# Attention with an MLP mixer on one core: score products over all 32 rows of a head slot, the exponent offset as a product of constants, a six-step VectorE exponential, set-up fills moved

## The chip, the cores and the metric

The kernel runs on one core of one Trainium2 chip. The metric is the device time of one execution in microseconds (us), as the median of several runs. A profile of one further execution gives the rows shown here; its time stands beside the median below. TensorE (PE) does the matrix products, ScalarE (ACT) and VectorE (DVE) work on their results, SyncE (SP) issues the transfers. TensorE's clock is granted in one of two levels, 1.2 and 2.4 GHz, which the profile writes as 0.5 and 1.0 of full speed.

## The reference

```python
xn = _layernorm(A_x)                                   # (1, 2048, 640) bf16
def _A_ref(x, wqkv, wo):                               # H = 32 heads of Dh = 20
    qkv = ((x @ wqkv).reshape(B, S, 3, H, Dh)).transpose(2, 0, 3, 1, 4)
    q, k, v = qkv[0], qkv[1], qkv[2]
    scores = jnp.einsum("bhqd,bhkd->bhqk", q, k) * (Dh ** -0.5)
    p = _softmax(scores, axis=-1)
    o = jnp.einsum("bhqk,bhkd->bhqd", p, v)
    return o.transpose(0, 2, 1, 3).reshape(B, S, D) @ wo
def _B_ref(x, w1, b1, w2, b2):                         # an MLP over the 2048 positions, 1536 wide
    h = _layernorm(x)
    u = _gelu(jnp.einsum("bsd,sf->bdf", h, w1) + b1)
    return (jnp.einsum("bdf,fs->bds", u, w2) + b2).transpose(0, 2, 1)
return A_x + _A_ref(xn, A_wqkv, A_wo) * _silu(_B_ref(xn, B_w1, B_b1, B_w2, B_b2))
```

## The kernel before

The 32 heads are worked in eight groups G of four. A group's q and k are made by products with `wqkvp_sb`, whose columns are spread so that each head has a slot of 32 rows in `qk_sb`: 20 rows of the head and 12 that hold whatever follows it in the weights. The step that takes them out of PSUM (`ev_fn`, L878 on VectorE, L877 on ScalarE in the first microseconds) multiplies and adds a number for each row (columns of `cst_sb`): it scales q, sets the spare rows of q and k to zero, and puts into the first spare row the constant 49152 (`OFFS`) on q's side and 1 on k's.

The attention is cut into 2048 units: a unit is one head, one block of 512 queries and one block of 128 keys. `emit_st` writes a unit's score product (L920): 128 keys by 512 queries into one PSUM bank, with the head's 20 rows as contraction. Two to five score products stand next to each other in the order, on different groups of 32 rows of the array, so that they run side by side. PSUM's eight banks: 0 to 2 and 3 and 4 are the two groups that ScalarE's exponential (L945) empties three or two units at a time into `pt_sb`; bank 5 is VectorE's; bank 6 collects the value products; bank 7 serves all other products.

About one unit in eleven has its exponential on VectorE. Its score product takes 21 rows, so that the constant adds 49152 to the score. VectorE then computes the exponential with seven instructions on 128 by 512 values (`start_dchain`, L984 to L991): it takes the low 16 bits of the score with its offset (`ew_sb`), builds a correction from them (`ev_sb`, `es_sb`, `el_sb`) and adds it to the score to give the bits of a bfloat16 number (`dpt_sb`). `emit_pv` writes the value products (L1025): the exponentials of a unit as moving operand, 32 columns of `v_sb` (a column of ones and the head's 20 values among them) as weights, four heads side by side.

Beside the attention run the MLP's products (L674), the products for later groups (L598), and near the end the output products (L736, L742). Their results leave PSUM on VectorE.

The order of instructions on every engine is fixed when the program is built. `schedule` simulates the engines with costs for each instruction and takes, step after step, the candidate that is ready first, by priority. It also keeps a model of TensorE's clock (`_Gate`): each product adds a number of columns to a running count, 512 for a full product, `512 * 0.156` for a score product and `512 * 0.25` for a value product, and where the count runs low the planner puts in products of constants whose result nobody reads (`warm_step`, L1387, operands from `wrm_sb`). Nothing of this model is known to the chip.

At the start VectorE fills constants: `wrm_sb`, bank 6, the identity, four small columns of `cst_sb`, the ones and gaps of `v_sb` (L499, L501), `on_sb` and `wo7_sb` (L502, L503; `wo7_sb` reads as `wo_sb` in rows of the profile). Then come the layer norm's statistics (L522, L524, L527).

Of the kernel before, what the change touches and what calls it, by code (L numbers as in the profile page):

```python
# [10 lines left out]
P = 128  # L11
# [28 lines left out]
class _Gate:  # L40
# [235 lines left out]
class _Kern:  # L276
# [6 lines left out]
    RP = 25  # L283
    VB = 724
# [36 lines left out]
    def build(self):  # L321
# [4 lines left out]
        with es:  # L326
# [20 lines left out]
            sb("wrm_sb", [P, 512], bf)  # L347
# [3 lines left out]
            sb("es_sb", [P, nd], bf)  # L351
# [25 lines left out]
    def schedule(self):  # L377
# [8 lines left out]
        ew_sb, ev_sb, es_sb, el_sb = t["ew_sb"], t["ev_sb"], t["es_sb"], t["el_sb"]  # L386
# [48 lines left out]
        def dma(fn, reads, writes, name, nbytes, tag=None):  # L435
            pr.dma(fn, reads=reads, writes=writes, name=name, cost=1800.0 + nbytes / 170.0)
# [24 lines left out]
        def small(fn):  # L461
            def f(e):
# [14 lines left out]
        pr.dve(lambda e: e.memset(wrm_sb[:], 1.0), writes=[S_("warm")], name="warm1", cost=240)  # L477
# [3 lines left out]
        selap = bass.AP(idf_sb, DH, [[P, P], [32, GH]])  # L481
        pr.dve(lambda e: e.tensor_reduce(cst_sb[:, 0:1], selap, mybir.AxisListType.X, ALU.add), reads=[S_("idf")],
               writes=[S_("bk")], name="bk", cost=150)
        CQ0 = self.LOG2E * 128.0 / math.sqrt(float(DH))
        pr.dve(lambda e: e.tensor_scalar(cst_sb[:, 1:2], cst_sb[:, 0:1], self.OFFS, None, ALU.mult),
               reads=[S_("bk")], writes=[S_("bq")], name="bq", cost=150)
        pr.dve(lambda e: e.tensor_scalar(cst_sb[:, 3:4], cst_sb[:, 0:1], -1.0, 1.0, ALU.mult, ALU.add),
               reads=[S_("bk")], writes=[S_("ck")], name="ck", cost=150)
        pr.dve(lambda e: e.tensor_scalar(cst_sb[:, 4:5], cst_sb[:, 0:1], -CQ0, CQ0, ALU.mult, ALU.add),
               reads=[S_("bk")], writes=[S_("cq")], name="cq", cost=150)  # L490
# [5 lines left out]

        for h0, nh in ((0, 8), (8, 24)):
            onesap = bass.AP(v_sb, voff(h0), [[NB * VB, P], [VB, NB], [22, nh], [21, 2]])
            pr.dve(lambda e, ap=onesap: e.memset(ap, 1.0), writes=[S_("v_ones")], name="v_ones", cost=100.0 + NB * nh * 2)  # L499
            gapap = bass.AP(v_sb, voff(h0 + nh - 1) + 22, [[NB * VB, P], [VB, NB], [1, 10]])  # L500
            pr.dve(lambda e, ap=gapap: e.memset(ap, 0.0), writes=[S_("v_ones")], name="v_gap", cost=240)  # L501
# [979 lines left out]
```

## Time and profile before

| | |
|---|---|
| median of 3 runs | 1028.91 us (1022.38 to 1039.81) |
| the profiled execution's own time | 1025.38 us |
| its span, from the first to the last instruction | 1023.6 us |
| mean granted clock of TensorE over the span | 0.851 |
| busy: TensorE, ScalarE, VectorE | 90%, 87%, 76% of the span |
| instructions | 15713 |

Busy shares are of the whole span. The kernel's stretches have different limits, so the rows below take stretches apart: one at the high clock level, one at the low level and some in between. A matrix product's busy time is modelled at its end and overlaps with its neighbours, so a busy TensorE may still have room.

### The profile page before, as it was taken

The numbers are of one execution on the slowest core, as the hardware profiler recorded it, in microseconds if no ns is written. First come the engines' busy times: TensorE is split into PE (matmuls) and PEld (weight loads), VectorE is DVE, ScalarE is ACT, GpSimd is POOL, SyncE is SP. The second block draws the span as 40 slices with busy tenths as digits, with TensorE's granted clock in tenths as the row PEclk, the third lists the DMA queues.
The fourth block names the chain that finished last, engine by engine and source line by source line (L and its number), as shares of the span: only waits on it lengthen the run. The fifth ranks groups of instructions, "written<-read, shape, count | busy, mean of one in ns | idle before, by whom it ended". The sixth has DMA issues, their size and how long they took to land.

```text
span 1023.6 us, 15713 instructions
## 1 busy us (share of the span) xinstructions
PE 916.9 (90%) x5972; PEld 273.8 (27%) x5972; DVE 779.8 (76%) x1874; ACT 887.9 (87%) x782; POOL 13.0 (1%) x31
## 2 busy tenths in 40 slices
PE   7889788899899898898999998888898899789997
PEld 4432222222222222222222222222222222322222
DVE  7878889867787878877658877886878767676665
ACT  3799999988999988998978989999999988787773
POOL 1400000000000000000000000000000000000000
PEclk9899999957989969988758889998989978885557
DMA  7030000000010101000020110101101012300001
GB/s 225 8 89 6 6 6 6 7 28 20 6 47 7 47 1 48 6 6 6 7 61 7 37 37 6 32 5 38 36 6 36 6 39 70 96 1 26 1 26 52
DMA packets 42203, 30.69 MB, mean 30 GB/s; under 512 B 4707, under 2 KB 41571, under 8 KB 42131
## 3 DMA queue, kind: packets, MB, share of 16 engines
q1 hardware_dynamic: 42131, 29.70, 9.7%
q8 instruction: 49, 0.80, 0.3%
q14 instruction: 23, 0.19, 0.1%
HBM read 23.40 MB, written 6.29 MB: 29 GB/s over the span
## 4 chain that ended last, share of the span: by engine, by line
PE 45%; DVE 28%; ACT 22%; issue 4%; POOL 0%; DVEq 0%; POOLq 0%
ACT pt_sb L945 21%; PE ps_all L920 15%; PE ps_all L1025 9%; PE ps_all L674 8%; DVE ew_sb L984 5%; PE ps_all L1387 5%; PE ps_all L598 4%; PE ps_all L736 4%; DVE dpt_sb L991 3%; DVE es_sb L987 3%; DVE qk_sb L878 3%; DVE el_sb L990 3%; DVE ev_sb L985 2%; DVE es_sb L989 2%; DVE el_sb L988 1%
## 5 line engine op out<-in xcount | busy, mean ns | idle before, releaser
L945 ACT ACTIVATE pt_sb<-ps_all 128x1536 bf16<-128x1536 f32 x743 | 863.1, 1257 | 103.8 <-PE ps_all L920 99.6
L920 PE MATMUL ps_all<-qk_sb 20*128 20x512 bf16 (+1 forms) x2048 | 358.6, 433 | 66.0 <-ACT pt_sb L945 35.7
L984 DVE TENSOR_SCALAR ew_sb<-ps_all 128x512 uint16<-128x512 uint16 x192 | 131.3, 684 | 132.3 <-PE ps_all L920 132.1
L1025 PE MATMUL ps_all<-pt_sb,v_sb 128*32 128x512 bf16 x1856 | 189.3, 441 | 0.0
L920 PEld LDWEIGHTS ps_all<-qk_sb 20*128 20x128 bf16 (+1 forms) x2048 | 82.7, 93 | 381.0 <-ACT pt_sb L945 209.0
L991 DVE SCALAR_TENSOR_TENSOR dpt_sb<-ps_all,el_sb 128x512 uint16<-128x512 f32 x192 | 132.2, 689 | 5.4
L1387 PE MATMUL ps_all<-wrm_sb 128*128 128x512 bf16 (+1 forms) x356 | 104.2, 404 | 11.4 <-DVE qk_sb L878 7.1
L598 PE MATMUL ps_all<-xnT_sb,wqkvp_sb 128*128 128x512 bf16 x320 | 101.4, 415 | 9.8 <-DVE wqk_sb L682 3.7
L674 PE MATMUL ps_all<-regB,regA 128*128 128x512 bf16 (+1 forms) x384 | 83.4, 341 | 4.8 <-DVE qk_sb L878 4.7
L990 DVE TENSOR_TENSOR el_sb<-es_sb,el_sb 128x512 bf16<-128x512 bf16 x192 | 81.5, 425 | 6.2
L987 DVE TENSOR_TENSOR es_sb<-ev_sb 128x512 bf16<-128x512 bf16 x192 | 81.1, 422 | 5.3
L1025 PE MATMUL ps_all<-dpt_sb,v_sb 128*32 128x512 bf16 x192 | 84.2, 446 | 0.0
L674 PE MATMUL ps_all<-regC,regA 128*128 128x128 bf16 (+1 forms) x384 | 80.6, 342 | 2.2 <-DVE qk_sb L878 2.2
L878 DVE TENSOR_SCALAR qk_sb<-ps_all,cst_sb 128x512 bf16<-128x512 f32 x60 | 48.2, 804 | 14.6 <-PE ps_all L598 14.5
L985 DVE TENSOR_SCALAR ev_sb<-ew_sb 128x512 bf16<-128x512 uint16 x192 | 55.4, 288 | 4.7
L989 DVE TENSOR_SCALAR es_sb<-es_sb 128x512 bf16<-128x512 bf16 x192 | 55.2, 287 | 0.0
L988 DVE TENSOR_SCALAR el_sb<-ev_sb 128x512 bf16<-128x512 bf16 x192 | 54.8, 285 | 0.0
L1025 PEld LDWEIGHTS ps_all<-pt_sb,v_sb 128*32 128x32 bf16 x1856 | 35.8, 97 | 67.5 <-issue 52.3
L1387 PEld LDWEIGHTS ps_all<-wrm_sb 128*128 128x128 bf16 x356 | 34.6, 111 | 62.6 <-DVE qk_sb L878 12.8
L736 PE MATMUL ps_all<-wo_sb,xnT_sb 120*128 120x512 bf16 (+3 forms) x160 | 44.6, 408 | 2.1 <-DVE regC L752 2.1
L674 PEld LDWEIGHTS ps_all<-regC,regA 128*128 128x128 bf16 x384 | 30.8, 111 | 46.5 <-issue 34.0
L598 PEld LDWEIGHTS ps_all<-xnT_sb,wqkvp_sb 128*128 128x128 bf16 x320 | 25.8, 101 | 64.5 <-issue 13.3
(68 smaller groups left out, 395.9 us busy)
## 6 DMA issues: line engine op xcount, KB each, us to landing
regA<-in_B_w_dram SPq DMA_DIRECT2D x6, 1024.0 KB
regA<-in_B_w_dram SPq DMA_DIRECT2D x8, 768.0 KB
regA<-in_A_x_dram SPq DMA_DIRECT2D x7, 640.0 KB
oT_scratch_dram<-stage_sb SPq DMA_DIRECT2D x28, 128.0 KB
xnT_sb<-oT_scratch_dram SPq DMA_DIRECT2D x4, 480.0 KB
out_dram<-regC SPq DMA_DIRECT2D x3, 640.0 KB
wqk_sb<-in_A_wqkv_dram SPq DMA_DIRECT2D x2, 800.0 KB
wv_sb<-in_A_wqkv_dram SPq DMA_DIRECT2D x1, 800.0 KB
```

The lines of the kernel that those rows point to most:

```text
L598: steps.append(("pe", lambda e, dc=dc: e.matmul(ps(bk), wqkvp_sb[:, dc, w, G, :], xnT_sb[:, dc, tb * 512:(tb + 1) * 512], start=(dc == 0), ...
L674: steps.append(("pe", lambda e, k=k: e.matmul(ps(bk, n), wap[:, k, col0:col0 + 128], rows[:, k, c0:c0 + n], start=(k == 0), stop=(k == nk ...
L736: steps.append(("pe", lambda e, c=c, k=k: e.matmul(ap, oT_sb[0:k, c, b * 128:(b + 1) * 128], wo_sb[0:k, c, c0:c0 + n], start=(c == 0), sto ...
L878: return lambda e: e.tensor_scalar(dst, src, sc, bias, ALU.mult, ALU.add)
L920: pr.pe(lambda e, outp=outp, lhsT=lhsT, rhs=rhs, g=g: e.matmul(outp, lhsT, rhs, start=True, stop=True, tile_position=(32 * g, 0)), reads=[ ...
L945: tk = pr.act(lambda e: e.activation(outp, inp, AF.Exp, scale=math.log(2.0) / 128.0), reads=[bank_slot[b] for b in banks[:n]], writes=[S_( ...
L984: (lambda e: e.tensor_scalar(w3, lo, 0x7FFF, None, ALU.bitwise_and), bs, [S_("ew")], dv(N)),
L987: (lambda e: e.tensor_tensor(s_, v_, v_, ALU.mult), [S_("ev")], [S_("es")], dv(N, .52)),
L990: (lambda e: e.tensor_tensor(l_, s_, l_, ALU.mult), [S_("es"), S_("el")], [S_("el")], dv(N, .52)),
L991: (lambda e: e.scalar_tensor_tensor(o_, zr, -(self.OFFS - 16256.0), l_, ALU.add, ALU.add), bs + [S_("el")], [S_(f"dpt{s0 + i}") for i in r ...
L1025: pr.pe(lambda e, outp=outp, lhsT=lhsT, rhs=rhs, k=k, g=g: e.matmul(outp, lhsT, rhs, start=(k == 0), stop=(k == NB - 1), tile_position=(0, ...
L1387: pe_full(lambda e: e.matmul(ps(wb, n), wrm_sb[:, 0:P], wrm_sb[:, 0:n], start=True, stop=True), [S_("warm")], [bank_slot[wb]], "warm", n)
```

## The change

Score products take all 32 rows of the slot (L910 of the changed kernel). Only q's spare rows are set to zero, by a scale without an addition; k's spare rows keep what the weights gave, and k is copied as it is. The offset of VectorE's units is written into bank 5 ahead of the score product by a full product of constants over 128 rows (`prime`, L1313): 128 rows of 1 by 128 rows of 49152/128. The score product then adds to it (`start=not dvex`). The planner takes a priming product when bank 5 is free, and a VectorE unit only in a primed bank.

VectorE's exponential becomes six steps: the correction is built as a product of two linear functions of `ew_sb` and of `ew_sb` itself, and `es_sb` is gone. One of its products now multiplies a bfloat16 by a 16-bit whole number.

The planner's model of the clock counts `512 * 0.25` columns for a score product. Its costs for transfers are other numbers as well (`DMA0`, `DMAB`). The fills of `v_sb`, `on_sb` and `wo7_sb` become jobs that the planner places after the first normalised blocks, and the first value products wait for the fill of `v_sb` (`c01`).

```diff
-            sb("wrm_sb", [P, 512], bf)
+            sb("wrm_sb", [P, P + 512], bf)
...
-        pr.dve(lambda e: e.memset(wrm_sb[:], 1.0), writes=[S_("warm")], name="warm1", cost=240)
+        pr.dve(lambda e: e.memset(wrm_sb[:, 0:P], 1.0), writes=[S_("warm1")], name="warm1", cost=100)
+        pr.dve(lambda e: e.memset(wrm_sb[:, P:P + 512], self.OFFS / P), writes=[S_("warm")], name="warm", cost=200)
...
-            return lambda e: e.tensor_scalar(dst, src, sc, bias, ALU.mult, ALU.add)
+            return lambda e: e.tensor_scalar(dst, src, sc, None, ALU.mult)
...
-                kk = DH + 1 if dvex else DH
-                lhsT = qk_sb[32 * g:32 * g + kk, slot, 1, c * 128:(c + 1) * 128]
-                rhs = qk_sb[32 * g:32 * g + kk, slot, 0, p * 512:(p + 1) * 512]
+                lhsT = qk_sb[32 * g:32 * g + 32, slot, 1, c * 128:(c + 1) * 128]
+                rhs = qk_sb[32 * g:32 * g + 32, slot, 0, p * 512:(p + 1) * 512]
...
+                    outp, lhsT, rhs, start=not dvex, stop=True, tile_position=(32 * g, 0)),
...
-            pr.gate.add(pr.T["pe"], n * 512 * 0.156)
+            pr.gate.add(pr.T["pe"], n * 512 * 0.25)
...
-                (lambda e: e.tensor_scalar(v_, w_, 1.0 / 256.0, -64.0, ALU.mult, ALU.add), [S_("ew")], [S_("ev")],
+                (lambda e: e.tensor_scalar(v_, w_, 1.0 / 256.0, -128.0, ALU.mult, ALU.add), [S_("ew")], [S_("ev")],
                  dv(N, .26)),
-                (lambda e: e.tensor_tensor(s_, v_, v_, ALU.mult), [S_("ev")], [S_("es")], dv(N, .52)),
-                (lambda e: e.tensor_scalar(l_, v_, a3, b3, ALU.mult, ALU.add), [S_("ev")], [S_("el")], dv(N, .26)),
-                (lambda e: e.tensor_scalar(s_, s_, -4096.0, None, ALU.add), [S_("es")], [S_("es")], dv(N, .26)),
-                (lambda e: e.tensor_tensor(l_, s_, l_, ALU.mult), [S_("es"), S_("el")], [S_("el")], dv(N, .52)),
+                (lambda e: e.tensor_scalar(l_, w_, a3 / 65536.0, (b3 - 64.0 * a3) / 256.0, ALU.mult, ALU.add),
+                 [S_("ew")], [S_("el")], dv(N, .26)),
+                (lambda e: e.tensor_tensor(l_, v_, l_, ALU.mult), [S_("ev"), S_("el")], [S_("el")], dv(N, .52)),
+                (lambda e: e.tensor_tensor(l_, l_, w_, ALU.mult), [S_("el"), S_("ew")], [S_("el")], dv(N, .52)),
...
+        add_job("consts", cs[:2] + [("tag", "c01")], ("xn_g0",), 21.0)
+        add_job("consts2", cs[2:], ("xn_g1",), 24.5)
...
+        def prime(dg):
+
+            for b in dg:
+                pe_full(lambda e, b=b: e.matmul(ps(b), wrm_sb[:, 0:P], wrm_sb[:, P:P + 512], start=True, stop=False),
+                        [S_("warm"), S_("warm1")], [bank_slot[b]], "offs", 512)
+            dgrp_state[dg] = "primed"
```

The planner gives a new order. Three places of it follow. The first is VectorE at the start of the program, from the last small constant to the layer norm's first statistics. Before:

```order
L491 MEMSET wqk_sb 128x8
L499 MEMSET v_sb 128x16x8x2
L501 MEMSET v_sb 128x16x5
L499 MEMSET v_sb 128x16x24x2
L501 MEMSET v_sb 128x16x5
L502 MEMSET on_sb 128x256
L503 MEMSET wo_sb 128x320
L522 BN_STATS bst_sb<-regA 128x6
```

The same place of the changed kernel, where L514 and L516 are the statistics:

```order
L489 TENSOR_SCALAR cst_sb<-cst_sb 128x1
L491 MEMSET wqk_sb 128x8
L514 BN_STATS bst_sb<-regA 128x6
L516 BN_STATS bst_sb<-regA 128x6
L519 BN_AGGR st_sb<-bst_sb 128x2
```

Six fills have left the stretch ahead of the statistics; they stand after the first normalised blocks and between later statistics.

The second place is VectorE's exponential of one unit in the middle of the program, without other work between. Before (L984 reads the scores, L991 writes the result):

```order
L984 TENSOR_SCALAR ew_sb<-ps_all 128x512
L985 TENSOR_SCALAR ev_sb<-ew_sb 128x512
L987 TENSOR_TENSOR es_sb<-ev_sb 128x512
L988 TENSOR_SCALAR el_sb<-ev_sb 128x512
L989 TENSOR_SCALAR es_sb<-es_sb 128x512
L990 TENSOR_TENSOR el_sb<-es_sb,el_sb 128x512
L991 SCALAR_TENSOR_TENSOR dpt_sb<-ps_all,el_sb 128x512
```

The changed kernel (L974 reads the scores, L981 writes the result):

```order
L974 TENSOR_SCALAR ew_sb<-ps_all 128x512
L975 TENSOR_SCALAR ev_sb<-ew_sb 128x512
L977 TENSOR_SCALAR el_sb<-ew_sb 128x512
L979 TENSOR_TENSOR el_sb<-ev_sb,el_sb 128x512
L980 TENSOR_TENSOR el_sb<-el_sb,ew_sb 128x512
L981 SCALAR_TENSOR_TENSOR dpt_sb<-ps_all,el_sb 128x512
```

One step on one operand is gone; the products of two operands are still two.

The third place is TensorE between the 1,817th and the 1,852nd score product, where neither the MLP nor the output has products ready. Before (L920 are score products, L1387 products of constants that nobody reads):

```order
L1025 MATMUL ps_all<-dpt_sb,v_sb 32x512
L920 MATMUL ps_all<-qk_sb 128x512 x2
L1387 MATMUL ps_all<-wrm_sb 128x512
L920 MATMUL ps_all<-qk_sb 128x512 x3
L1387 MATMUL ps_all<-wrm_sb 128x512
L1387 MATMUL ps_all<-wrm_sb 128x256 x16
L920 MATMUL ps_all<-qk_sb 128x512 x6
```

The changed kernel (L910 are score products, L1398 products that nobody reads, L1313 priming products of bank 5):

```order
L910 MATMUL ps_all<-qk_sb 128x512 x3
L1398 MATMUL ps_all<-wrm_sb 128x512
L910 MATMUL ps_all<-qk_sb 128x512 x2
L1398 MATMUL ps_all<-wrm_sb 128x512
L1313 MATMUL ps_all<-wrm_sb 128x512
L910 MATMUL ps_all<-qk_sb 128x512 x4
L1015 MATMUL ps_all<-pt_sb,v_sb 32x512 x5
```

The bursts of sixteen half-width products are gone, and priming products stand in between. Counted over the whole order of TensorE, the products that nobody reads fall from 207 of 512 columns and 149 of 256 to 111 and 42, and 189 priming products of 512 columns come in. VectorE's units are 192 before and 189 now; ScalarE has 371 exponentials of three units before and 372 now, and 371 of two units in both. Other products keep their number.

## Rows read from the trace of the kernel before

**Rows 1.** The page's first part: busy us of each engine over the span.

```profile
PE 916.9 (90%) x5972; PEld 273.8 (27%) x5972; DVE 779.8 (76%) x1874; ACT 887.9 (87%) x782; POOL 13.0 (1%) x31
```

**Rows 2.** Span and mean granted clock of the core.

```profile
core 0: 1023.6 us, clock 0.851
```

**Rows 3.** The span in 40 slices: granted clock of TensorE in tenths.

```profile
PEclk9899999957989969988758889998989978885557
```

**Rows 4.** Stretches of the span: length, busy us (instructions) by engine, granted clock, DMA.

```profile
64.00:192.00 128.00, 110.95 (x789) 31.08 (x788) 111.66 (x258) 123.55 (x109) 0.00 (x0) 1.00 0.02 6
192.00:804.00 612.00, 553.53 (x3655) 159.86 (x3652) 470.47 (x1119) 555.87 (x492) 0.00 (x0) 0.86 0.08 22
804.00:930.00 126.00, 111.38 (x716) 34.25 (x714) 91.74 (x222) 107.70 (x95) 0.00 (x0) 0.81 0.14 43
930.00:1010.00 80.00, 78.78 (x370) 17.98 (x367) 49.03 (x117) 57.24 (x47) 0.00 (x0) 0.50 0.05 17
```

**Rows 5.** Score products (L920) alone, same view: PE, weight loads, granted clock.

```profile
64.00:192.00 128.00, 47.05 (x300) 11.82 (x299) 1.00 0.02 6
320.00:352.00 32.00, 12.26 (x78) 3.29 (x78) 1.00 0.14 38
640.00:704.00 64.00, 23.28 (x146) 5.93 (x146) 1.00 0.10 30
930.00:1010.00 80.00, 30.57 (x133) 5.20 (x130) 0.50 0.05 17
```

**Rows 6.** Waits of ScalarE and TensorE: us in total, times, longest.

```profile
ACT pt_sb L945 <- PE ps_all L920: 99.6, 124, 2.3
PE ps_all L920 <- DVE dpt_sb L991: 25.5, 55, 1.9
```

**Rows 7.** Waits of ScalarE within 930 to 1010 us.

```profile
ACT pt_sb L945 <- PE ps_all L920: 21.7, 24, 1.6
```

**Rows 8.** TensorE's groups of instructions within 930 to 1010 us.

```profile
L920 PE MATMUL ps_all<-qk_sb 20*128 20x512 bf16 (+1 forms) x133 | 31.1, 604 | 0.0
L736 PE MATMUL ps_all<-wo_sb,xnT_sb 120*128 120x512 bf16 (+2 forms) x83 | 28.1, 470 | 1.2 <-DVE regC L752 1.2
```

**Rows 9.** Groups by form over the whole span: busy us, mean ns, idle before.

```profile
L945 ACT ACTIVATE pt_sb<-ps_all 128x1536 bf16<-128x1536 f32 x371 | 545.7, 1471 | 78.2 <-PE ps_all L920 75.8
...
L920 PE MATMUL ps_all<-qk_sb 20*128 20x512 bf16 x1856 | 324.0, 433 | 39.1 <-ACT pt_sb L945 35.7 <-DVE es_sb L987 0.5 <-ACT qk_sb L877 0.3
...
L991 DVE SCALAR_TENSOR_TENSOR dpt_sb<-ps_all,el_sb 128x512 uint16<-128x512 f32 x192 | 132.2, 689 | 5.4
L984 DVE TENSOR_SCALAR ew_sb<-ps_all 128x512 uint16<-128x512 uint16 x192 | 131.3, 684 | 132.3 <-PE ps_all L920 132.1
...
L920 PE MATMUL ps_all<-qk_sb 21*128 21x512 bf16 x192 | 83.6, 436 | 26.9 <-DVE dpt_sb L991 25.5
L990 DVE TENSOR_TENSOR el_sb<-es_sb,el_sb 128x512 bf16<-128x512 bf16 x192 | 81.5, 425 | 6.2
L987 DVE TENSOR_TENSOR es_sb<-ev_sb 128x512 bf16<-128x512 bf16 x192 | 81.1, 422 | 5.3
...
L985 DVE TENSOR_SCALAR ev_sb<-ew_sb 128x512 bf16<-128x512 uint16 x192 | 55.4, 288 | 4.7
L989 DVE TENSOR_SCALAR es_sb<-es_sb 128x512 bf16<-128x512 bf16 x192 | 55.2, 287 | 0.0
L988 DVE TENSOR_SCALAR el_sb<-ev_sb 128x512 bf16<-128x512 bf16 x192 | 54.8, 285 | 0.0
```

**Rows 10.** Timeline of the first 21 us on VectorE, TensorE and ScalarE: start, us, instruction.

```profile
2.37 0.07 DVE L491 MEMSET wqk_sb<- 128x8 uint32 x1
...
6.37 0.43 DVE L522 BATCH_NORM_STATS2 bst_sb<-regA 128x6 f32<-128x320 bf16 x1
...
16.52 2.32 PE L598 MATMUL ps_all<-xnT_sb,wqkvp_sb 128*128 128x512 bf16 x10
...
20.15 6.88 ACT L945 ACTIVATE pt_sb<-ps_all 128x1536 bf16<-128x1536 f32 x6 [0.21 <-PE ps_all L920]
```

More of the change, by code (lines that the diff above doesn't have):

```diff
@@ L53, in __init__ @@
         self.hist = []
+        self.allrec = []
     def at(self, t):
@@ L283 @@
     RP = 25
+    DMA0 = 2000.0
+    DMAB = 330.0
     VB = 724
@@ L435, in dma @@
         def dma(fn, reads, writes, name, nbytes, tag=None):
-            pr.dma(fn, reads=reads, writes=writes, name=name, cost=1800.0 + nbytes / 170.0)
+            pr.dma(fn, reads=reads, writes=writes, name=name, cost=self.DMA0 + nbytes / self.DMAB)
             if tag:
@@ L480, in schedule @@
                cost=200)
[L481 to L483 removed]
+        selap = bass.AP(idf_sb, DH, [[P, P], [32, GH], [1, 32 - DH]])
+        pr.dve(lambda e: e.tensor_reduce(cst_sb[:, 0:1], selap, mybir.AxisListType.XY, ALU.add), reads=[S_("idf")],
+               writes=[S_("pad")], name="pad", cost=150)
         CQ0 = self.LOG2E * 128.0 / math.sqrt(float(DH))
[L485 to L488, printed above, removed]
         pr.dve(lambda e: e.tensor_scalar(cst_sb[:, 4:5], cst_sb[:, 0:1], -CQ0, CQ0, ALU.mult, ALU.add),
[L490 removed]
+               reads=[S_("pad")], writes=[S_("cq")], name="cq", cost=150)
         pr.dve(lambda e: e.memset(wqk_sb[:, 6400:6416], 0.0), writes=[S_("wq_end")], name="wqe", cost=80)
@@ L495, in voff @@
             return 22 * h + (10 if h >= 8 else 0)
[L497 to L501, printed above, removed]
-        pr.dve(lambda e: e.memset(on_sb[:], 0.0), writes=[S_("on")], name="on0", cost=250)
-        pr.dve(lambda e: e.memset(wo7_sb[:], 0.0), writes=[S_("wo7")], name="wo70", cost=300)
         def st(k, b0, nb):
@@ L601, in make @@
                 dst = qk_sb[:, slot, w, tb * 512:(tb + 1) * 512]
-                steps.append(("ev", dst, ps(bk), "k" if w else "q", None, [bank_slot[bk], S_("bk"), S_("bq"), S_("ck"), S_("cq")],
+                steps.append(("ev", dst, ps(bk), "copy" if w else "q", None, [bank_slot[bk], S_("cq")],
                               [S_(f"qkb{slot}_{w}_{tb}")], f"qke{G}_{w}_{tb}", 512))
@@ L1254, in pe_cands @@
                 for dg in self.DVE_GROUPS:
-                    if dgrp_state[dg] == "free" and dve_room(len(dg)) and all(fin_bank(b) for b in dg):
+                    if dgrp_state[dg] == "free" and all(fin_bank(b) for b in dg) and nxt[0] + self.DVE_TAIL_GUARD < NU:
+                        c.append((3.0, pr.ready("pe", [S_("warm"), S_("warm1")], [bank_slot[b] for b in dg]),
+                                  lambda dg=dg: prime(dg)))
+                        break
+                    if dgrp_state[dg] == "primed" and dve_room(len(dg)):
                         c.append((4.0, pr.ready("pe", [], [bank_slot[b] for b in dg]), lambda dg=dg: do_st_dve(dg)))
@@ L1326, in do_st @@
                 for dg in self.DVE_GROUPS:
-                    if dgrp_state[dg] == "free" and len(us) + len(dg) <= 4 and dve_room(len(dg)) \
-                            and all(fin_bank(b) for b in dg) \
+                    if dgrp_state[dg] == "primed" and len(us) + len(dg) <= 4 and dve_room(len(dg)) \
                             and pr.ready("pe", [], [bank_slot[b] for b in dg]) <= T:
```

35 lines of the change are left out of this document (21 added, 14 removed).

## The prediction

> **What bounds the kernel now.** I read the busy shares first [rows 1]: TensorE 90%, ScalarE 87%, VectorE 76%. None is full, so the bound must change with the place. The mean granted clock, 0.851 [rows 2], is the first thing that does: in 40 slices it stands at full speed for some and falls to half in others, three slices on end near the finish [rows 3]. So I took stretches apart by clock [rows 4]. From 64 to 192 us the clock is 1.00, ScalarE is busy 123.55 of 128 us (97%), TensorE 110.95 (87%), VectorE 111.66 (87%): there ScalarE's exponentials are the bound, and nothing that TensorE or VectorE saves can shorten it. From 930 to 1010 us the clock is 0.50, TensorE is busy 78.78 of 80 us, ScalarE 57.24 (72%) and VectorE 49.03: there TensorE is the bound, and ScalarE waits 21.7 us for score products [rows 7], out of 99.6 us over the span [rows 6].
>
> What the low level costs is read from the score products, of which each of the 2048 units has one [rows 5]. At the high level 300 + 78 + 146 = 524 in 128 + 32 + 64 = 224 us, which is 2.34 for each us; at the low level 133 in 80, which is 1.66. A microsecond at the low level does 0.71 of the work, so it loses 0.29. The share of time at the low level is (1 - 0.851) / 0.5 = 0.298 of 1023.6, or 305 us. It costs 305 x 0.29 = 88 us. A run that is at the high level throughout would have a span of about 935 us.
>
> **What the clock follows.** TensorE's busy time does not decide it. It is busy 98% from 930 to 1010 us at the low level, and 87% from 64 to 192 us at the high one [rows 4]. In the first of these the largest item is score products, 31.1 us of TensorE's time [rows 8], 20 rows each in two to five at once; two or three of them, the usual number in the order, fill 40 or 60 of the array's 128 rows. The other large items there fill most of it (output products over 120 rows). So what I take from the rows is that a partly filled array goes with the low level, and that the rows that a score product leaves empty are the place where filling costs nothing: 20 rows take 433 ns and 21 rows 436 [rows 9], so 32 rows should take as long. That filled rows count, beside busy time, no row here proves; I give it 0.88.
>
> The Trainium skill, in "TensorE: Matmul & The Clock Gate", under "What's actually happening", says that the clock is set by how busy the engine has been lately. Taken as busy time alone, these rows speak against it; taken word for word it makes the wider score products worth nothing for the clock, and that is the first rival below.
>
> **The change part by part.** *Score products over 32 rows, and the planner's fewer idle products.* The planner counts a score product higher, and spends some of the count. From the order, the full-array products (all but score and value) come to 676,608 columns before and 696,832 now, the priming products among them. To this the score products add 12 of 128 rows, worth 6,144 full columns for each 128 of them. So fifteen of sixteen blocks of 128 units gain, by 3,600 to 13,200 where most had 35,000 to 43,500. The exception is one: between the 1,793rd and the 1,920th the full columns fall from 38,400 to 32,256, by just the 6,144 that the rows bring. Filling there stays what it was. I keep all the low time of the place that this block lies in, 804 to 930 us: (1 - 0.81) / 0.5 x 126 = 48 us [rows 4]. Of the other 257 us I keep one in seven, 37 us; none is left if each fall of the clock has gone, and as much as before if rows don't count. Together 85 us, at 0.29 each 25 us in place of 88. **Gain 63 us**; ends 0 and 88.
>
> *Priming products.* 189 of 512 columns come in. A full product of 512 columns takes 0.23 us in a row of ten at the high level (2.32 us, [rows 10]), so 43 us. What leaves is 96 idle ones of 512 (22 us) and 107 of half the width (12 us). Net 9 us of TensorE over the span. At the high level they lie beside ScalarE's work, since TensorE has 17 us to spare in 128 [rows 4]; without that cover they would cost the 9. In the 85 us at the low level they take about 9 / 1000 x 85 x 2 = 1.5 us. **Cost 1 us.** A priming product waits for bank 5, which VectorE's last step frees, and everything behind it on TensorE waits as well, ScalarE's next score products among it. Before, the unit's score product stood in the same place and waited for the same step, 25.5 us in 55 waits [rows 6]; I take that as unchanged, and double it in a rival.
>
> *VectorE's exponential.* The seven steps take 684 + 288 + 422 + 285 + 287 + 425 + 689 = 3080 ns [rows 9], 591 us for 192 units. Six steps with the prices of their like: 684 + 288 + 285 + 425 + 425 + 689 = 2796 ns, 528 us for 189. The second product mixes bfloat16 and whole numbers, which no product does in this trace; reading whole numbers cost a one-operand step nothing (288 against 285 ns), so I take 425 ns. The far bound is 689, the step that reads PSUM; then VectorE saves 13 us instead of 63. VectorE is 87% busy where ScalarE sets the pace [rows 4], so **neither end moves the sum**. It would matter if VectorE rose over ScalarE, which neither price brings about. Copying k rather than scaling it is nothing for the same reason.
>
> *ScalarE.* One exponential of three units more, 1.47 us [rows 9]: **cost 1.5 us.**
>
> *Fills at the start.* The statistics begin at 6.37 us without a wait [rows 10]; the small constants end at 2.44. So up to 3.9 us could go, if the first block of x has landed by then, which no row shows. What comes later in the way: two fills stand between the first normalised block and the first score product, and eleven v products that stood behind q's and k's now stand ahead of them. Bounds -3.9 to +1 us, **I take -2**, since the first exponential at 20.15 us [rows 10] hangs on VectorE's chain of statistics. SP's queue keeps its transfers in the same order until then.
>
> **Sum.** 1023.6 - 63 + 1 + 1.5 - 2 = 961 us of span. The profiled execution's own time lies 1.8 us above its span (1025.4), so 963 us. The median of the runs, 1028.9, lies 3.5 above that execution, within a spread of 1022 to 1040; I leave this to the range. About 2% is also what a measurement of this kernel can tell from no change.
>
> **The rivals.**
>
> *The clock follows busy time, rows count nothing.* Filling then changes by the full columns alone, 3%. The low time stays at 305 us, and in it TensorE is the bound and pays for the priming: 9 x 0.3 x 2 = 5 us. 1025.4 + 5 + 1.5 - 2 = 1030 us. For it: nothing in the trace separates rows from columns. Against: the busiest stretch has the lowest clock. Chance 0.07.
>
> *Rows count nothing, and the planner has spent the credit* (the slower side). The block from the 1,793rd to the 1,920th unit has lost 6,144 full columns. If the clock then stays low through it, its 128 units take 128 / 1.66 = 77 us; at the mean of that place, 1 - 0.29 x 0.38 = 0.89 of the full rate, they take 128 / 2.08 = 61.5. That is 15 us on the 1030, 1045 us. It decides from the point at which less than the lost columns comes back from the rows. Chance 0.05.
>
> *The priming product holds TensorE up.* If the 25.5 us of waits double and each of 55 late ones adds its own 0.23 us, 25.5 + 13 = 38 us fall on the path: 963 + 38 = 1001 us. For it: VectorE's jobs come late by whatever the planner's costs miss. Against: VectorE has fewer steps to do. Chance 0.08.
>
> *Nearly no low time is left.* One in seven becomes nothing and 804 to 930 us recovers too: 1025.4 - 88 + 0.5 = 938 us. For it: 64 to 192 us is at the high level throughout already with the old filling. Against: the place without a gain in columns. Chance 0.12.
>
> **How the numbers follow.** The forecast has the remaining 0.68, between 945 and 990 us. The range from 936 to 1001 us takes it in, with most of the near-floor case and the case of held-up priming; at 1001 about 215 us would still be low. Outside stay the cases in which rows count nothing (0.12), a time under 936 and one over 1001 from a longer held-up case, about 2 in 10 together. Faster by over 2% (under 1008 us) is 0.68 + 0.12 + 0.08, 0.88; within 2% the first rival and the lower half of the second, 0.09; slower 0.03.
>
> **What would show it.** Right: a mean clock of 0.94 to 0.97; 930 us onward no longer at 0.50; ScalarE 97% busy through most stretches and its wait for score products (99.6 us) halved; score products of about 435 ns; VectorE's busy time down by some 60 us; statistics that begin before 4 us. Wrong: a mean clock near 0.85 at the same score counts; a wait of priming products for VectorE's last step well over 25 us; the mixed product at 0.69 us with VectorE near 97% where the clock is high.

## The result and the profile after

| | before | changed kernel |
|---|---|---|
| median | 1029.05 us (1022.38 to 1039.81) | 953.32 us (944.52 to 955.36) |
| profiled execution, its span | 1025.38, 1023.6 us | 955.36, 953.5 us |
| mean granted clock over the span | 0.851 | 0.961 |

The ratio of the times is 0.9268, with a 95% interval from 0.9182 to 0.9354: 76 us faster, where 963 us was forecast from a range of 936 to 1001. A kernel's runs differ by up to several per cent, the longer ones at a lower granted clock, so "near its fastest" below means within 1.5% of a kernel's fastest run, and comparisons go by those runs.

The page of the changed kernel, first its busy us by engine (as [rows 1]), then the granted clock in 40 slices (as [rows 3]) and the chain that ended last by engine:

```profile
PE 807.9 (85%) x5853; PEld 257.5 (27%) x5958; DVE 734.7 (77%) x1663; ACT 881.3 (92%) x783; POOL 13.9 (1%) x31
...
PEclk9879999999799999999978998899999999999999
...
DVE 43%; PE 33%; ACT 13%; issue 10%; POOL 0%; DVEq 0%; POOLq 0%
```

The three slices at half clock near the end are gone. TensorE's busy time fell by 109 us, though its order has only 14 products fewer (5,958 for 5,972): a product at the high level is shorter, and 105 products have no record in this trace. Low time is now (1 - 0.961) / 0.5 x 953.5 = 74 us, against 305. The third line is the surprise, and the experiments come back to it: the chain runs through VectorE and TensorE, and ScalarE, busy 92%, has 13% of it.

Stretches of the changed kernel (columns as in [rows 4]):

```profile
0.00:64.00 64.00, 50.94 (x341) 24.73 (x347) 44.29 (x132) 36.45 (x35) 13.93 (x31) 0.84 0.45 123
...
64.00:192.00 128.00, 110.25 (x780) 32.16 (x794) 102.33 (x219) 124.46 (x109) 0.00 (x0) 1.00 0.03 8
192.00:804.00 612.00, 524.70 (x3805) 161.36 (x3867) 473.41 (x1053) 583.99 (x520) 0.00 (x0) 0.96 0.08 23
804.00:880.00 76.00, 60.13 (x460) 18.03 (x466) 56.88 (x129) 74.98 (x68) 0.00 (x0) 1.00 0.22 69
880.00:940.00 60.00, 53.36 (x413) 16.91 (x420) 49.55 (x114) 59.50 (x54) 0.00 (x0) 1.00 0.07 23
...
480.00:512.00 32.00, 29.19 (x163) 7.92 (x166) 20.14 (x45) 27.42 (x25) 0.00 (x0) 0.68 0.14 41
```

From 804 to 940 us the clock is 1.00 and ScalarE is busy 99%. The low time that is left lies mostly at the start ((1 - 0.84) / 0.5 x 64 = 20 us) and in the middle (the last line: 20 us more).

Groups by form of the changed kernel (as [rows 9]):

```profile
L935 ACT ACTIVATE pt_sb<-ps_all 128x1536 bf16<-128x1536 f32 x372 | 548.2, 1474 | 34.7 <-PE ps_all L910 31.9
L910 PE MATMUL ps_all<-qk_sb 32*128 32x512 bf16 x2048 | 324.0, 396 | 67.1 <-ACT pt_sb L935 42.9 <-DVE dpt_sb L981 10.5 <-DVE wqk_sb L674 3.8
L981 DVE SCALAR_TENSOR_TENSOR dpt_sb<-ps_all,el_sb 128x512 uint16<-128x512 f32 x189 | 130.3, 690 | 5.5
L974 DVE TENSOR_SCALAR ew_sb<-ps_all 128x512 uint16<-128x512 uint16 x189 | 130.0, 688 | 135.7 <-PE ps_all L910 132.8
...
L979 DVE TENSOR_TENSOR el_sb<-ev_sb,el_sb 128x512 bf16<-128x512 bf16 x189 | 80.2, 425 | 6.2
L980 DVE TENSOR_TENSOR el_sb<-el_sb,ew_sb 128x512 bf16<-128x512 bf16 x189 | 80.1, 424 | 5.9
L1313 PE MATMUL ps_all<-wrm_sb 128*128 128x512 bf16 x150 | 59.7, 398 | 34.4 <-DVE dpt_sb L981 32.2
L975 DVE TENSOR_SCALAR ev_sb<-ew_sb 128x512 bf16<-128x512 uint16 x189 | 54.7, 290 | 4.8
L977 DVE TENSOR_SCALAR el_sb<-ew_sb 128x512 bf16<-128x512 uint16 x189 | 54.0, 285 | 0.0
```

A score product over 32 rows takes 396 ns in the mean, not more than the 433 of 20 rows [rows 9]. The mean is lower since more of them are at the high level: from 64 to 192 us, where both kernels are at 1.00, the two lines below give 385 ns for 20 rows and 384 for 32.

```profile
L920 PE MATMUL ps_all<-qk_sb 20*128 20x512 bf16 x270 | 41.8, 385 | 4.8 <-ACT pt_sb L945 4.4 <-DVE es_sb L987 0.3
L910 PE MATMUL ps_all<-qk_sb 32*128 32x512 bf16 x299 | 45.1, 384 | 9.2 <-DVE dpt_sb L981 5.6 <-ACT pt_sb L935 2.8 <-DVE rden_sb L1042 0.3
```

The mixed product (L980) takes 424 ns, the value that was taken, and the six steps 2802 ns. (150 of the 189 priming products have a record.) The Trainium skill, in "VectorE: DVE Perf Modes", under "What auto-detection actually checks", asks for the faster mode of a product of two operands only that every tensor is 16 bits wide with a step of one element. The 424 ns agree with that, against 425 for the product of two bfloat16 operands (L979).

Waits of the changed kernel (as [rows 6]):

```profile
ACT pt_sb L935 <- PE ps_all L910: 37.1, 66, 3.1
PE ps_all L1313 <- DVE dpt_sb L981: 32.2, 70, 1.3
...
PE ps_all L910 <- DVE dpt_sb L981: 10.5, 15, 1.4
```

ScalarE's wait for score products fell by 62.5 us, from 99.6, and its busy time by 6.6 [rows 1]; together that is 69.1 of the 70.1 us that the span lost. TensorE's wait for VectorE's last step did not fall: 32.2 + 10.5 us against 25.5.

The ramp of the changed kernel (timeline, as [rows 10]):

```profile
3.09 0.49 DVE L514 BATCH_NORM_STATS2 bst_sb<-regA 128x6 f32<-128x320 bf16 x1 [0.60 <-DMA regA<-in_A_x_dram]
...
14.64 2.73 PE L609 MATMUL ps_all<-wv_sb,xnT_sb 128*128 128x160 bf16 x20 [2.83 <-DVE bst_sb L516]
...
17.36 3.55 PE L590 MATMUL ps_all<-xnT_sb,wqkvp_sb 128*128 128x512 bf16 x10
...
22.39 1.45 ACT L935 ACTIVATE pt_sb<-ps_all 128x1536 bf16<-128x1536 f32 x1 [2.08 <-PE ps_all L910]
```

The statistics begin 3.3 us earlier, now held only by x's arrival. But twenty v products stand ahead of q's and k's ten, which take 3.55 us in place of 2.32, and the first exponential begins 2.2 us later.

### The profile page after: what moved, and what is told of

The parts are those of the page before. It is cut to its first block, busy times and chain, and to the rows that moved or that the text cites. A ratio compares the mean times of both kernels' runs of the same rounds, so it can differ in the third digit from the quotient of the medians.

```text
span 953.5 us, 15629 instructions
## 1 busy us (share of the span) xinstructions
PE 807.9 (85%) x5853; PEld 257.5 (27%) x5958; DVE 734.7 (77%) x1663; ACT 881.3 (92%) x783; POOL 13.9 (1%) x31
## 3 DMA queue, kind: packets, MB, share of 16 engines
q1 hardware_dynamic: 42131, 29.70, 10.5%
## 4 chain that ended last, share of the span: by engine, by line
DVE 43%; PE 33%; ACT 13%; issue 10%; POOL 0%; DVEq 0%; POOLq 0%
ACT pt_sb L935 13%; PE ps_all L910 13%; DVE ew_sb L974 9%; DVE dpt_sb L981 7%; DVE el_sb L979 6%; PE ps_all L1015 5%; PE ps_all L666 5%; DVE el_sb L980 5%; PE ps_all L1313 4%; DVE ev_sb L975 4%; DVE el_sb L977 3%; PE ps_all L590 2%; PE ps_all L728 2%; DVE wqk_sb L674 1%; DVE stage_sb L1049 1%
## 5 line engine op out<-in xcount | busy, mean ns | idle before, releaser
L935 ACT ACTIVATE pt_sb<-ps_all 128x1536 bf16<-128x1536 f32 x744 | 857.2, 1261 | 40.1 <-PE ps_all L910 37.1
L910 PE MATMUL ps_all<-qk_sb 32*128 32x512 bf16 x2048 | 324.0, 396 | 67.1 <-ACT pt_sb L935 42.9
L974 DVE TENSOR_SCALAR ew_sb<-ps_all 128x512 uint16<-128x512 uint16 x189 | 130.0, 688 | 135.7 <-PE ps_all L910 132.8
L910 PEld LDWEIGHTS ps_all<-qk_sb 32*128 32x128 bf16 x2048 | 80.5, 91 | 296.6 <-ACT pt_sb L935 193.7
L981 DVE SCALAR_TENSOR_TENSOR dpt_sb<-ps_all,el_sb 128x512 uint16<-128x512 f32 x189 | 130.3, 690 | 5.5
L1313 PE MATMUL ps_all<-wrm_sb 128*128 128x512 bf16 x150 | 59.7, 398 | 34.4 <-DVE dpt_sb L981 32.2
L979 DVE TENSOR_TENSOR el_sb<-ev_sb,el_sb 128x512 bf16<-128x512 bf16 x189 | 80.2, 425 | 6.2
L980 DVE TENSOR_TENSOR el_sb<-el_sb,ew_sb 128x512 bf16<-128x512 bf16 x189 | 80.1, 424 | 5.9
L666 PE MATMUL ps_all<-regB,regA 128*128 128x128 bf16 (+1 forms) x372 | 72.9, 311 | 5.3 <-DVE qk_sb L869 2.4
L977 DVE TENSOR_SCALAR el_sb<-ew_sb 128x512 bf16<-128x512 uint16 x189 | 54.0, 285 | 0.0
L1398 PE MATMUL ps_all<-wrm_sb 128*128 128x512 bf16 (+1 forms) x139 | 42.0, 385 | 5.7 <-DVE ps_all L482 2.2
L1313 PEld LDWEIGHTS ps_all<-wrm_sb 128*128 128x128 bf16 x189 | 18.2, 96 | 96.2 <-DVE dpt_sb L981 89.5
L666 PEld LDWEIGHTS ps_all<-regB,regA 128*128 128x128 bf16 x384 | 27.2, 101 | 45.4 <-issue 25.7
L609 PE MATMUL ps_all<-wv_sb,xnT_sb 128*128 128x160 bf16 (+1 forms) x160 | 32.0, 313 | 4.8 <-DVE bst_sb L516 2.8
```

Of the source, the lines that this page charges most:

```text
L666: steps.append(("pe", lambda e, k=k: e.matmul(ps(bk, n), wap[:, k, col0:col0 + 128], rows[:, k, c0:c0 + n], start=(k == 0), stop=(k == nk ...
L910: pr.pe(lambda e, outp=outp, lhsT=lhsT, rhs=rhs, g=g, dvex=dvex: e.matmul(outp, lhsT, rhs, start=not dvex, stop=True, tile_position=(32 * ...
L935: tk = pr.act(lambda e: e.activation(outp, inp, AF.Exp, scale=math.log(2.0) / 128.0), reads=[bank_slot[b] for b in banks[:n]], writes=[S_( ...
L974: (lambda e: e.tensor_scalar(w3, lo, 0x7FFF, None, ALU.bitwise_and), bs, [S_("ew")], dv(N)),
L977: (lambda e: e.tensor_scalar(l_, w_, a3 / 65536.0, (b3 - 64.0 * a3) / 256.0, ALU.mult, ALU.add), [S_("ew")], [S_("el")], dv(N, .26)),
L979: (lambda e: e.tensor_tensor(l_, v_, l_, ALU.mult), [S_("ev"), S_("el")], [S_("el")], dv(N, .52)),
```

## The experiments

Each kernel is the changed kernel with the edit shown, unless it says otherwise. Ratios are against the kernel before, measured on the same chip; three chips were used, and its median on them was 1024.41, 1027.56 and 1028.97 us.

**Rows back to 20, same order.** Every instruction stays where it is; the score products take 20 rows.

```diff
-                lhsT = qk_sb[32 * g:32 * g + 32, slot, 1, c * 128:(c + 1) * 128]
-                rhs = qk_sb[32 * g:32 * g + 32, slot, 0, p * 512:(p + 1) * 512]
+                lhsT = qk_sb[32 * g:32 * g + DH, slot, 1, c * 128:(c + 1) * 128]
+                rhs = qk_sb[32 * g:32 * g + DH, slot, 0, p * 512:(p + 1) * 512]
```

> The changed kernel with score products over 20 rows again, the order of every instruction unchanged. Theory, filled rows hold the clock up: the granted clock falls from 0.96 to 0.83 to 0.88 and the time rises to 1000 to 1035 us, most of the gain. Rival, the clock follows busy time or the new order alone brings the gain (priming products, better placed idle ones): clock 0.95 or more, 945 to 960 us.

Measured: 1044.14 us in the median. Its runs spread from 1012.37 to 1074.89 us, so no interval is given. The fastest, at a clock of 0.871 over a span of 1010.6 us, is within the expected range and still 59 us above the changed kernel. The profiled run (span 1049.6 us) has 0.821. Two stretches of it and ScalarE's wait:

```profile
64.00:192.00 128.00, 112.75 (x672) 28.40 (x683) 90.52 (x191) 110.56 (x96) 0.00 (x0) 0.81 0.02 5
890.00:970.00 80.00, 77.30 (x357) 15.96 (x362) 46.13 (x104) 61.10 (x51) 0.00 (x0) 0.50 0.15 47
```

```profile
ACT pt_sb L935 <- PE ps_all L910: 115.9, 146, 2.2
```

The order is the same, and only the rows differ. The late stretch is at 0.50, where TensorE is busier (97%) than the 32-row kernel is near there at 1.00 (89%, 880 to 940 us above); the kernel before is busy 98% at 0.50 too [rows 4]. So filled rows make the difference, and the rival by which the clock follows busy time alone is out. (The 0.81 from 64 to 192 us is not in every run with 20 rows: the kernel before [rows 4] and the corrected plan with 20 rows, below, have 1.00 there.) The rows are filled with zeros on q's side, so rows whose products are all zero count. The price holds too: in the fastest run low time is 261 against 74 us, 187 x 0.29 = 54 us, and the spans differ by 57.

**Old count of the planner's clock model**, so that it puts in more idle products (93,184 columns, against 67,584).

```diff
-            pr.gate.add(pr.T["pe"], n * 512 * 0.25)
+            pr.gate.add(pr.T["pe"], n * 512 * 0.156)
```

> The changed kernel with the planner's old count for a score product (0.156 of a full one), rows still 32, so that the planner puts in more idle products (93,184 columns for 67,584). Theory, filled rows hold the clock up and TensorE has room: clock 0.97 to 0.99, 938 to 953 us. Rival, the planner's new count is itself part of the gain because idle products cost time: 960 us or more with a clock that is no higher.

Measured: 960.71 us, 0.9325 [0.925, 0.940], clock 0.969 in the profiled run. The clock is no worse and the time no better, so the few microseconds that the theory expected of filling the rest didn't come. The median lies on the rival's side, by which idle products cost time, but the interval overlaps that of the changed kernel, and neither is shown. ScalarE's wait is 44.8 us, against 37.1.

**Both: 20 rows and the old count.**

> Both undone: 20 rows and the old count, with the priming products, the six steps and the moved fills kept. Theory, filled rows hold the clock up: clock 0.85 to 0.90, 990 to 1025 us, a little under the run with 20 rows and the new count, since the idle products that the new count dropped are back. Rival, the rest of the change brings the gain: 945 to 965 us.

Measured: 1014.97 us in the median of 998.05 to 1038.41, 0.9736 [0.9646, 0.9826], clock 0.874 in the profiled run (1026.85 us). With 20 rows the old count has a lower median by some 30 us and a lower fastest run by 14, which the spread of both covers; with 32 rows it brings nothing. Filling by idle products didn't replace the rows: by the runs near each kernel's fastest (1000.6 and 958.5 us) they are worth 42 us here too.

**One more VectorE step in each unit, not planned.** It computes into a tile that nobody reads; the order stays.

```diff
-                (lambda e: e.tensor_scalar(l_, w_, a3 / 65536.0, (b3 - 64.0 * a3) / 256.0, ALU.mult, ALU.add),
+                (lambda e: (e.tensor_scalar(t["es_sb"][:, 0:N], w_, 1.0 / 256.0, -128.0, ALU.mult, ALU.add),
+                            e.tensor_scalar(l_, w_, a3 / 65536.0, (b3 - 64.0 * a3) / 256.0, ALU.mult, ALU.add))[1],
```

> The changed kernel with one more one-operand step on VectorE in each of its 189 units (into a spare tile that nobody reads, 0.285 us each, 54 us in all), the planned order unchanged otherwise. Theory, VectorE is off the path: 951 to 959 us. Rival, the shorter exponential is part of the gain because VectorE's last step holds up the priming product: 970 us or more, with a longer wait of L1313's successor for dpt_sb.

Measured: 1005.02 us in the median, 0.9752 [0.967, 0.9834]. The runs near its fastest have 1002.20 us, 49 more than the changed kernel. The added steps are 189 x 0.285 = 54 us; since they overlap their neighbours, VectorE's busy time rises by 38 (773.0 against 734.7), on an engine that is busy 77%. This felled the view that VectorE's time is hidden. From the profiled run (1012.51 us) its chain by engine, its wait, and its score products in the stretch at the high level, of which the changed kernel has 299 (below):

```profile
DVE 47%; PE 35%; issue 10%; ACT 6%; POOL 1%; DVEq 0%; POOLq 0%
```

```profile
PE ps_all L1315 <- DVE dpt_sb L983: 50.1, 83, 1.5
```

```profile
64.00:192.00 128.00, 42.90 (x287) 10.70 (x287) 1.00 0.02 6
```

The chain of waits of the changed kernel shows the cause (start, us, what):

```profile
161.12 0.70 DVE ew_sb L974
...
161.85 0.29 DVE ev_sb L975
162.14 0.21 DVE el_sb L977
...
162.38 0.43 DVE el_sb L979
...
162.84 0.43 DVE el_sb L980
...
163.29 0.70 DVE dpt_sb L981
...
164.04 0.39 PE ps_all L1313
164.43 0.33 PE ps_all L910
...
164.78 0.70 DVE ew_sb L974
```

This is a ring through bank 5: VectorE's six steps (2.87 us from start to end), the priming product (0.39), the score product (0.33), and the next unit's first step, 3.66 us later. VectorE can't begin the next unit while TensorE has its part; it fits in other steps where it has them, and then waits. From 64 to 192 us 13 of 28 rounds take 3.63 to 3.71 us, so this is the shortest that the ring allows, and with the extra step 12 of 26 take 3.83 to 3.92. One of those:

```profile
161.77 0.69 DVE L975 TENSOR_SCALAR ew_sb<-ps_all 128x512 uint16<-128x512 uint16 x1 [0.84 <-PE ps_all L911]
...
165.64 0.69 DVE L975 TENSOR_SCALAR ew_sb<-ps_all 128x512 uint16<-128x512 uint16 x1 [0.23 <-PE ps_all L911]
```

VectorE's waits for score products (132.8 us) and its busy time (734.7) are 867 of 953.5 us, 91%, not 77%. This share is a hint only: it is 88% in the run truecost below (129.5 and 684.4 of 921.9), where the ring has left the chain. What is added inside such a ring has little to hide behind, and the hold-up shows in the clock too: the runs near its fastest have clocks of 0.926 to 0.954, against 0.956 to 0.983. In the one of 1002.20 us (0.943, span 1000.4) low time is 114 us, 40 more, worth 12 of the 47 us between the spans.

**The same step, planned**: the diff above with the third step's cost doubled, so that the planner knows of it.

```diff
-                 [S_("ew")], [S_("el")], dv(N, .26)),
+                 [S_("ew")], [S_("el")], 2.0 * dv(N, .26)),
```

> The same extra step on VectorE as in the run before (0.285 us in each unit, result unread), but the planner is told of it, so that the order is made for it (183 VectorE units in place of 189). Theory, what hurt was that VectorE's last step came later than the order allows, with TensorE standing at the priming product: 950 to 970 us, and 64 units at the high clock in 27 to 28 us. Rival, VectorE's length itself sets the pace: 985 us or more.

Measured: 952.85 us, 0.9288 [0.9209, 0.9367], as the changed kernel. The planner gives VectorE 183 units in place of 189 and another order; from 64 to 192 us 10 of 28 rounds still take 3.86 to 3.92 us. So a longer chain need not cost time. That the price is for a chain longer than the plan fits this run; whether fewer units or their places did it is not separated.

**No priming product.** Its place in the order and its wait stay. Left out is the offset of VectorE's units, so their exponentials are other numbers.

```diff
-                    outp, lhsT, rhs, start=not dvex, stop=True, tile_position=(32 * g, 0)),
+                    outp, lhsT, rhs, start=True, stop=True, tile_position=(32 * g, 0)),
...
-                pe_full(lambda e, b=b: e.matmul(ps(b), wrm_sb[:, 0:P], wrm_sb[:, P:P + 512], start=True, stop=False),
-                        [S_("warm"), S_("warm1")], [bank_slot[b]], "offs", 512)
+                pe_full(None, [S_("warm"), S_("warm1")], [bank_slot[b]], "offs", 512)
```

> The changed kernel without the 189 priming products; the wait for bank 5 stays at its place in TensorE's order and all else is in the same order. It leaves the offset out, so VectorE's units get wrong exponentials. Theory, the priming products are 14% of the full columns and hold the clock up: clock 0.88 to 0.94, 965 to 1000 us. Rival, they are time that TensorE must find: clock as before, 935 to 948 us.

Measured: 936.98 us, 0.9115 [0.9063, 0.9166], 16 us faster than the changed kernel, though the clock fell from 0.961 to 0.934. Chain by engine, and the score products of the stretch at the high level:

```profile
ACT 47%; DVE 23%; PE 22%; issue 8%; POOL 0%; DVEq 0%; POOLq 0%
```

```profile
64.00:192.00 128.00, 47.17 (x313) 12.17 (x310) 0.99 0.04 12
```

Both theories were half right. The priming products do hold the clock up: low time goes from 74 to 124 us, 50 x 0.29 = 14 us. By this sum, leaving them out gives back those 14 and 16 more, an estimate of some 30 us gross of the 189 x 0.39 = 74 that they lie in the ring. 313 score products pass from 64 to 192 us, 287 with the extra step: the ring sets the rate where the clock does not. Its shortest round is 0.31 us shorter than the 3.66 of the changed kernel (11 of 28 take 3.31 to 3.43 us):

```profile
159.20 0.69 DVE L974 TENSOR_SCALAR ew_sb<-ps_all 128x512 uint16<-128x512 uint16 x1 [0.48 <-PE ps_all L910]
...
162.55 0.69 DVE L974 TENSOR_SCALAR ew_sb<-ps_all 128x512 uint16<-128x512 uint16 x1
```

**VectorE's steps planned nearer to what they take** (truecost). The costs beside the steps are 75 ns and 1.04, 0.52 or 0.26 for each of 512 elements, 2314 ns for the six; the trace has 2802, and 2.87 us from start to end. 70 ns more for each step:

```diff
-            dchain.extend((x, us, s0, grp) for x in ch)
+            dchain.extend(((x[0], x[1], x[2], x[3] + 70.0), us, s0, grp) for x in ch)
```

> The changed kernel with the planner's cost of each step of VectorE's exponential raised by 70 ns, to what the trace shows for the six (2.87 us); the planner then gives VectorE 170 units and ScalarE 19 more. Theory, the order expects VectorE too early: the wait of priming products for VectorE's last step falls from 32.2 to under 15 us and the clock rises over 0.97, against some 9 us more on ScalarE: 940 to 955 us. Rival, the lateness is harmless in this order: wait and clock as they are, 955 to 965 us from ScalarE's extra units.

Measured: 918.75 us, 0.8961 [0.8921, 0.9000], 35 us faster than the changed kernel with the same work in each unit, 170 of VectorE's units in place of 189, idle products of 72,704 columns in place of 67,584, and a clock of 0.980. Its chain and waits:

```profile
ACT 86%; PE 7%; issue 4%; DVE 2%; POOL 0%; DVEq 0%; POOLq 0%
```

```profile
ACT pt_sb L935 <- PE ps_all L910: 14.3, 14, 3.1
...
PE ps_all L1313 <- DVE dpt_sb L981: 3.5, 14, 0.4
```

The ring has gone from the chain and ScalarE has 86% of it, with 19 units more to do; from 64 to 192 us only 3 of 24 rounds are within 0.1 us of the shortest. Low time fell by 37 us, worth 11 of the 32 us of span; the other 21 are put down to the ring, as what is left. The gain was larger than either theory allowed.

**The same plan with 20 rows** (both diffs):

> The kernel whose planner knows VectorE's real step times (918.75 us), with score products over 20 rows, the order unchanged. Theory, filled rows hold the clock up whatever the order: clock 0.83 to 0.90 in place of 0.98, 970 to 1010 us. Rival, the rows mattered only because VectorE's lateness left TensorE standing and the clock near its fall: clock 0.95 or more, 920 to 935 us.

Measured: 982.19 us, 0.9587 [0.9499, 0.9675], clock 0.885. Against truecost the rows are worth 63 us; low time is 225 against 37 us, 188 x 0.29 = 55, and the spans (978.7, 921.9) differ by 57. The rows' gain is there without the ring, and in runs that lie close together (980.47 to 992.51 and 917.74 to 923.70 us).

**The kernel before, with 70 ns more for each of its seven steps** (the same edit):

> The kernel before with the planner's cost of each of the seven VectorE steps raised by 70 ns (169 VectorE units in place of 192), nothing else. Theory, lateness of VectorE is a cost of its own beside the clock: the wait of score products for dpt_sb falls from 25.5 to under 10 us, and the time to 985 to 1015 us, with the clock still at 0.83 to 0.90. Rival, the lateness came in only with the priming products: 1020 to 1040 us.

Measured: 971.29 us, 0.9451 [0.9377, 0.9526], clock 0.926, VectorE's units 169. So 58 us of the kernel before hung on the planner's cost of these steps: TensorE's wait for L991 is 3.8 us there, against 25.5 [rows 6]. Most of it came by the clock, which the expectation had left at 0.83 to 0.90: low time falls from 305 to 143 us, 162 x 0.29 = 47. What raised the clock is not separated. TensorE is held up less, and the new plan also puts in more idle products (166,400 columns, against 144,128). Against this run the changed kernel on the corrected plan with 20 rows (982.19 us, above) is no faster: apart from the rows, the change shows no gain there.

**The fills back at the start**, ahead of the statistics (the loop of `v_sb`'s fills, `on0` and `wo70`; the jobs are dropped):

```diff
-        add_job("consts", cs[:2] + [("tag", "c01")], ("xn_g0",), 21.0)
-        add_job("consts2", cs[2:], ("xn_g1",), 24.5)
...
+        pr.dve(lambda e: e.memset(on_sb[:], 0.0), writes=[S_("on")], name="on0", cost=250)
+        pr.dve(lambda e: e.memset(wo7_sb[:], 0.0), writes=[S_("wo7")], name="wo70", cost=300)
+        done.add("c01")
+        done.add("consts")
```

> The changed kernel with the fills of v_sb, on_sb and wo7_sb back at the start of VectorE's program. Theory, the moved fills start the statistics 3 us earlier but the first exponential hangs on q's and k's products, which stood behind eleven more v products: first exponential at 20 to 22 us in place of 22.4, time 948 to 962 us, no difference that can be told. Rival, moving them is worth its 3 us: first exponential at 24 to 26 us and 955 us or more.

Measured: 949.23 us, 0.9243 [0.9194, 0.9293]. The planner gives a new order here too (188 of VectorE's units). The first exponential begins at 20.17 us again, and no difference can be told: the intervals overlap.

**Fills back, on the truecost plan:**

> The kernel whose planner knows VectorE's real step times, with the fills back at the start of VectorE's program. Theory, the first exponential comes 2 to 4 us earlier (19.5 to 21.5 us for 23.8) and the rest is as it was: 914 to 920 us. Rival, the later fills are the better place: 921 us or more.

Measured: 917.58 us, 0.8937 [0.8879, 0.8994], clock 0.99. The first exponential begins at 19.91 us, against 23.77; the time is 1 us lower. Nearly 4 us at the start came to next to nothing, in an order that has more idle products (83,712 columns, against 72,704).

**More idle products on that**, `WARM_OVER` being the mark of the clock model to which the planner fills:

```diff
-    WARM_OVER = 3300.0
+    WARM_OVER = 3600.0
```

> The same with the planner's aim for TensorE's filling raised from 3300 to 3600, which puts in somewhat more idle products (88,320 columns for 83,712). Theory, what low time is left (a clock of 0.98) goes and idle products are free beside ScalarE: clock 0.985 to 0.995, 910 to 918 us. Rival, idle products take time from score products: 919 us or more.

Measured: 909.18 us, 0.8854 [0.8788, 0.8921], clock 0.993, the fastest of all, as the theory expected or a little better. VectorE also has 175 units here in place of 170, so idle products are not the only difference. Its busy line and ScalarE's wait (the lines of this kernel stand ten further down, L945 for L935):

```profile
PE 803.4 (88%) x5873; PEld 257.0 (28%) x5977; DVE 697.1 (77%) x1578; ACT 875.0 (96%) x789; POOL 13.4 (1%) x31
```

```profile
ACT pt_sb L945 <- PE ps_all L920: 7.6, 12, 1.9
```

ScalarE is busy 96% and waits 7.6 us for scores: this order is near what its exponentials alone take.

## Why the prediction was right, step by step

*What the low level costs, and that filled rows count.* Both held. 231 us less of low time at 0.29 are 67 of the 70.1 us of span that went. The three pairs with one order and 20 or 32 rows show it apart from all else. The spans differ by 57 us where the price gives 54 (rows20), by 57 where it gives 55 (truecost_rows20), and with the old count, in the runs of 1003.09 and 958.54 us, by 45 where 134 us of low time give 39.

*How much low time stays.* The size was right (74 us for 85), its places were not. The forecast kept 48 us from 804 to 930 us, because the columns of the block from the 1,793rd to the 1,920th unit come out even; the clock is 1.00 there. It kept 37 elsewhere; there are 74. That the two add up so nearly is luck. Counting an empty row like an idle column was no guide to the place. What the chip counts, no run settles.

*Priming products, 1 us.* Mis-sized: 16 us net in this order, by estimate 30 without what they do for the clock. The step that failed is "at the high level they lie beside ScalarE's work, since TensorE has 17 us to spare in 128". The spare was TensorE's, but the products stand in bank 5's ring, between VectorE's last step and its next. "Nothing that TensorE or VectorE saves can shorten it", said of 64 to 192 us, fell with it: 313 score products pass there without the priming products. Over the stretch at the high level the change as a whole still comes out even, 300 score products before [rows 5] and 299 after:

```profile
64.00:192.00 128.00, 44.92 (x299) 11.19 (x296) 1.00 0.03 8
```

A round of the ring on the kernel before takes 3.55 us, and its seven steps 3.07 from start to end:

```profile
151.79 0.69 DVE L984 TENSOR_SCALAR ew_sb<-ps_all 128x512 uint16<-128x512 uint16 x1
...
154.17 0.69 DVE L991 SCALAR_TENSOR_TENSOR dpt_sb<-ps_all,el_sb 128x512 uint16<-128x512 f32 x1
...
155.34 0.69 DVE L984 TENSOR_SCALAR ew_sb<-ps_all 128x512 uint16<-128x512 uint16 x1
```

The priming adds 0.31 us to a round (3.66 against 3.35 without it), and the dropped step takes 0.20 off (3.07 to 2.87). So the shortest round went from 3.55 to 3.66 us only.

So the sum held, in part by luck, because two terms that it put at about nothing nearly cancel: leaving out 0.31 us gave 16 us in one run, and adding 0.21 (3.87 for 3.66) cost 49 in another. That they balance is read from these rounds; no run measured the dropped step on the old order. The rival of held-up priming (38 us, 1001) named the right place and priced it too high.

*VectorE, "neither end moves the sum".* This fell. The six steps took what was forecast, but the far price of the mixed product, 689 ns, would have been 265 ns more in each round, more than the 0.21 us that the extra step adds to the shortest one, and that cost 49 us at an unchanged order. So the far price would have moved the sum; no run has it. The share of busy time hid it: the waits inside the ring belong to VectorE's bound as well. The Trainium skill, in "Perfetto Trace Analysis", under "Identifying the Most-Contended Engine", says to improve the engine with the highest occupancy first. Here that is ScalarE with 92%; the trace puts 13% of the chain on it, and the runs moved the time by VectorE's ring.

*ScalarE's 1.5 us* can't be told from the rest. *Fills, -2 us*: the statistics moved as forecast, but the first exponential came 2.2 us later, since the v products ahead of q and k, which the working named, cost more than the earlier start gave; the runs with the fills put back show that neither sign reaches the end measurably.

*Signs.* The clock (0.961), 930 us onward at 1.00, ScalarE's wait more than halved, statistics at 3.09 us came as written; score products at 396 ns are shorter than the 435 written; VectorE's busy time fell by 45 us, not 60, since the dropped step had overlapped its neighbours (0.20 us of a unit, not 0.28). The wrong sign "a wait of priming products well over 25 us" came with 32.2, and was the one to follow.

**Open.** Why the old count, with more idle products, is not faster with 32 rows: its order differs in many places. How far the 58 and 35 us of the corrected costs are due to fewer units on VectorE, to later places for them and to more idle products: the planner changes all three at once. How much of the 16 us without priming is slack that the plan kept for it.

## What to carry to other kernels

Where a product leaves rows of the array empty and takes as long with them filled, fill them, with zeros if need be: here that was worth 42 to 63 us of some 1000 at an unchanged order. An engine that is busy 77% can still set the pace when its steps and another engine's alternate through one buffer: look at the time from one round to the next, or add a step and see. In an order written ahead, compare each planned cost with the trace, and first of chains of dependent steps: 2.31 us planned for 2.87 and 2.52 for 3.07 were corrected here, and the new plans were 35 and 58 us faster.

## What was not expected of the hardware

Rows that multiply zeros hold the clock up: 0.871 (the fastest run) to 0.961, and 0.885 to 0.980, at one order each. And a hold-up of TensorE by a fraction of a microsecond for each unit costs twice, once as a wait and once by the clock: at one order the extra step took it from 0.956 to 0.983 down to 0.926 to 0.954. The corrected costs took it from 0.851 to 0.926 on the kernel before, with more idle products in the plan.
